# Wider stretches in a channel mix: one row of 512-column stretches over all batches, and a token mix cut 512, 512, 64

## The chip, the cores and the metric

The kernel runs on one core of one Trainium2 chip. The metric is the device time of one execution in microseconds; the median of three runs stands for a kernel. TensorE is called PE below, VectorE DVE, ScalarE ACT, GpSimd POOL, and SyncE, which issues the transfers, SP.

## What is computed

A linear attention whose feature map is a product of two small projections, followed by an MLP mixer (4 batches, 4 heads, 1088 tokens, 32 per head, so 128 channels):

```python
def phi(x):                                   # r = 8, r*r = 64 features
    a = np.einsum('rd,bhsd->bhsr', S1, x)
    b = np.einsum('rd,bhsd->bhsr', S2, x)
    return np.einsum('bhsi,bhsj->bhsij', a, b).reshape(*x.shape[:-1], r * r)
q_p, k_p = phi(q), phi(k)
kv = np.einsum('bhsf,bhsd->bhfd', k_p, v);  z = np.sum(k_p, axis=2)
x = num / den                                 # q_p @ kv over q_p @ z + 1e-6, as (batch, 1088, 128)

h = np.maximum(x.transpose(0, 2, 1) @ w_tok1, 0.0) @ w_tok2    # 1088 -> 256 -> 1088
u = x + h.transpose(0, 2, 1)
h2 = np.maximum(u @ w_ch1, 0.0) @ w_ch2                        # 128 -> 1536 -> 128
return u + h2
```

The weights arrive as 64-bit doubles.

## The kernel before, in words

**Numbers.** The doubles come in as pieces (`pieces[w, i]`, w = 0, 1 for the two token weights, 2, 3 for the two channel weights). `convert` turns a piece into 32-bit words: ACT splits off two parts into scratch tiles `c` and `tail` (512 columns, 4 buffers each), DVE takes three steps (L424, L428, L431), POOL adds (L435 `whole`, L437). `divide_weight` then makes a high half (ACT, L524) and a low half (POOL, L527) in `halves`. Most matmuls work on such halves: three matmuls, high x high, low x high, high x low, in place of one. Batch 0's token mix uses the unsplit words in full precision (L866, L988) and needs no halves.

**Work of one batch.** `keys`: projections of k (L554), products on DVE (L584), sums over tokens (L601). `queries_on_pe` (batch 0) or `queries_by_dma` (the others; projection L747, a way through DRAM, products on POOL L790). `mixing`: attention (L810), division on DVE, the split of x into `xh` (ACT, L834) and `xl` (POOL, L838), the first token weight (L866 or L872), relu, a transpose (L906), and the second token weight by chunks of columns, `CHUNKS`: 384, 384 and 320 (L988 for batch 0, on top of the transposed x of L897; L992 for the others, with the sum `us` made on DVE, L1008, from x transposed through DRAM). `evict` splits the sum u into `uh` (ACT, L963) and `ul` (DVE or POOL, L966).

**Channel mix.** The columns of u are taken in stretches, `SPANS`. Batch 0 has three of its own, the chunks; the other 3264 columns are one row of seven stretches of 384, one of 320 and one of 256, which may cross from one batch into the next. A stretch i has 12 blocks, one for each 128 of the 1536 hidden channels. A block is: `U{i}.f`, three matmuls into a `ps_h` bank (L1042); relu on ACT into `hh` (L1046); the low half `hl` on DVE (L1049); `U{i}.s`, three matmuls that add into a `ps_o` bank (L1055). After the last block DVE adds u (L1074, L1080) and SP stores. `SEGS` says in which order batch 0's blocks of its three stretches follow each other. All `.f` are in one fixed order, and all `.s`. Four `hid` buffers, three `ps_h`, two `ps_o` and four `u` buffers lie between the steps; a stretch is `WIDE` = 384 columns at most.

**Order.** `Plan` is a list scheduler that runs while the kernel is built: each operation has a cost for each engine that can do it, and among those that could start first, the one of highest level is emitted next. The level is the longest chain of costs behind it, plus `BOOST` by batch, plus a hand-set rank in `LEAD`. Where the plan sees PE without work, `fill` puts in 128-wide dummy matmuls on `ident` (L396). Buffers are modelled by `Hold`s. SP issues all transfers in the emitted order, at first in that of `LOADS`.

Of the kernel before, what the change touches and what calls it, by code (L numbers as in the profile page):

```python
# [10 lines left out]
F32R = mybir.dt.float32r  # L11
# [7 lines left out]
P = 128  # L19
# [8 lines left out]
CHUNKS = ((0, 384), (384, 384), (768, 320))  # L28
# [5 lines left out]
LOADS = "k0 q0 00 v0 01 02 03 04 10 11 20 30 q1 12 13 k1 21 31 v1 14 15 22 32".split()  # L34


WIDE = 384


def _spans():  # L40
    spans = [((0, c0, cn),) for c0, cn in CHUNKS]
    at = S
    for n in (384,) * 7 + (320, 256):
        parts = []
        while n:
# [11 lines left out]
SEGS = ((0, 0, 3), (1, 0, 3), (0, 3, 6), (1, 3, 6), (0, 6, 12), (1, 6, 12), (2, 0, 12))  # L57
assert sorted((i, e) for i, a, z in SEGS for e in range(a, z)) == [(i, e) for i in range(len(CHUNKS)) for e in range(NCH)]
# [7 lines left out]
    "A0.d0": -55300.0,  # L66
    "A0.d2": -2900.0,
    "A0.hT": 99500.0,
    "A0.n0": 59800.0,
    "A0.u1": 66400.0,  # L70
    "A0.u2": 63900.0,
    "A0.ul00": 51100.0,
    "A0.w2": 98700.0,
    "A0.x0": 29300.0,
    "A1.t0": -21500.0,
    "A1.t2": 16200.0,
    "A1.w0": -1423700.0,
    "A1.w2": 149000.0,
    "A1.x": 36300.0,
    "A2.n0": 110900.0,  # L80
    "A2.n1": 30300.0,
    "A2.n2": 115300.0,
    "A2.t2": -9900.0,
    "A2.uh05": -52300.0,
    "A2.uh06": -48100.0,
    "A2.w1": -147500.0,
    "A2.w2": -7500.0,
    "A3.hT": 82300.0,
    "A3.n0": 18000.0,
    "A3.t1": 40600.0,  # L90
    "A3.t2": 52300.0,
    "A3.uh09": 12800.0,
    "A3.us1": 38200.0,
    "A3.w0": -35900.0,
    "A3.w1": 2000.0,
    "A3.xb": -47500.0,
    "K0.c0": 184300.0,
    "K0.kvz": -17600.0,
    "K0.s14": 36100.0,
    "K0.s18": 52100.0,  # L100
    "K0.v8": -11500.0,
    "K1.c0": 73400.0,
    "K1.c8": -25000.0,
    "K1.p": 67100.0,
    "K1.s": 38100.0,
    "K1.v4": -86800.0,
    "K1.v8": -128900.0,
    "K2.p": -75625.5,
    "K2.s": 10700.0,
    "K3.p": 82600.0,  # L110
    "Q0.a00": 152400.0,
    "Q0.a01": 23200.0,
    "Q0.a11": -165700.0,
    "Q0.a20": 154800.0,
    "Q0.b01": 29200.0,
    "Q0.b11": -8100.0,
    "Q0.b21": 27500.0,
    "Q0.p0": 54300.0,
    "Q0.p2": 48700.0,
    "Q1.m00": 6600.0,  # L120
    "Q1.m01": -5000.0,
    "Q1.m10": 32900.0,
    "Q1.m11": -14900.0,
    "Q1.p": 2300.0,
    "Q2.p": 10200.0,
    "Q3.p": -69800.0,
    "U0.f": 780300.0,
    "U0.ol": 14800.0,
    "U1.f": 96700.0,
    "U1.oh": 52400.0,  # L130
    "U10.f": 900.0,
    "U11.f": 1400.0,
    "U2.f": -4000.0,
    "U4.f": 1480700.0,
    "U5.f": 163600.0,
    "U6.f": 150900.0,
    "U7.f": 35100.0,
    "w00.hi": -193600.0,
    "w00.lo": -296700.0,
    "w00.low": 6200.0,  # L140
    "w01.hi": -700.0,
    "w01.lo": -62200.0,
    "w02.clamp": 45400.0,
    "w02.lo": -1516300.0,
    "w02.low": 60300.0,
    "w02.shift": -5600.0,
    "w03.abs": -1200.0,
    "w03.add": -25300.0,
    "w03.hi": -52900.0,
    "w03.lo": -45700.0,  # L150
    "w03.merge": -189600.0,
    "w04.abs": 70300.0,
    "w04.clamp": 120900.0,
    "w04.hi": -95600.0,
    "w04.lo": -148800.0,
    "w04.low": 12100.0,
    "w04.merge": -96000.0,
    "w10.abs": 40900.0,
    "w10.hi": 9100.0,
    "w10.low": 19600.0,  # L160
    "w10.merge": 60000.0,
    "w11.abs": 27600.0,
    "w11.clamp": 23000.0,
    "w11.hi": -196900.0,
    "w11.lo": 183000.0,
    "w11.low": -2900.0,
    "w11.shift": -682900.0,
    "w12.abs": 42900.0,
    "w12.hi": -107800.0,
    "w12.lo": -27700.0,  # L170
    "w12.low": 159700.0,
    "w12.merge": 3100.0,
    "w13.abs": 21600.0,
    "w13.add": 1100.0,
    "w13.clamp": -55300.0,
    "w13.hi": 23500.0,
    "w14.clamp": 17900.0,
    "w14.lo": 33800.0,
    "w14.low": -113600.0,
    "w15.abs": -800.0,  # L180
    "w15.clamp": 34000.0,
    "w15.low": -82500.0,
    "w20.abs": 10900.0,
    "w20.add": -18200.0,
    "w20.low": 4400.0,
    "w21.abs": -10800.0,
    "w21.clamp": 74900.0,
    "w21.lo": -14000.0,
    "w22.lo": 4700.0,
    "w22.low": -175100.0,  # L190
    "w30.abs": -6400.0,
    "w30.lo": 12000.0,
    "w30.merge": 75500.0,
    "w30.shift": -68200.0,
    "w31.abs": -10200.0,
    "w31.clamp": 3800.0,
    "w31.hi": 16200.0,
    "w32.abs": -5300.0,
    "w32.add": 3600.0,
    "w32.clamp": 700.0,  # L200
    "w32.low": -289100.0,
# [140 lines left out]
def act_sb(n):  # L342
    return {"act": 100 + 0.834 * n}
# [15 lines left out]
def attn_mixer_kernel(ctx: ExitStack, tc: tile.TileContext, qT, kT, v1, s64, wt1, wt2, wc1, wc2, out):  # L359
# [46 lines left out]

    def convert(name, raw, n, loaded, dst=None, keep=None):
# [7 lines left out]
        def magnitude(_):  # L415
            t["c"] = const.tile([P, n], I32, name="s_c") if keep else new("c", [P, CONV], I32)[:, :n]
            nc.scalar.activation(f32(t["c"]), f32(high), AF.Abs)  # L417

        def rest(_):
            t["tail"] = new("tail", [P, CONV], I32)[:, :n]  # L420
            nc.scalar.activation(t["tail"], low.bitcast(U32), AF.Copy, scale=2.0 ** -29)  # L421
# [28 lines left out]
    for w, (src, sizes) in enumerate((  # L450
        (wt1, [n * DTOK for n in CUTS[0]]), (wt2, [cn for _, cn in CHUNKS for _ in range(2)]), (wc1, [n * P for n in CUTS[2]]), (wc2, [n * P for n in CUTS[3]]),
    )):
        for i, n in enumerate(sizes):
            pieces[w, i] = src[:, sum(sizes[:i]):sum(sizes[:i + 1])]
# [209 lines left out]
    def queries_on_pe(qp_hold):  # L664
# [16 lines left out]
        for g, (c0, cn) in enumerate(CHUNKS):  # L681
# [112 lines left out]
    def mixing(b, kvz_done, qp_done, qp_hold, boost, free):  # L794
# [5 lines left out]
        for g in range(3):  # L800
# [49 lines left out]
            if b:  # L850
                m = plan.add(f"{n}.h{g}", act_sb(384), high, [m], [xs_hold] if g == 0 else (), [x_hold] + ([xs_hold] if g else []), boost, order=split[:1])
                m = plan.add(f"{n}.l{g}", either(384), low, [m], (), [x_hold, xs_hold], boost, port=True)
# [37 lines left out]
        def residual(i, after):  # L890
# [10 lines left out]
            return plan.add(f"{n}.u{i}", {"pe": 3 * 109.0}, emit, [divided[i]], [u_banks[i]], [x_hold], boost, order=after)  # L901
# [75 lines left out]
        for i, (c0, cn) in enumerate(CHUNKS):  # L977
# [3 lines left out]
            def second(_, i=i, c0=c0, cn=cn):  # L981
# [4 lines left out]
                for f in range(2):  # L986
                    if not b:
                        nc.tensor.matmul(u_ps[:, :cn], lhsT=t["hTh"][:, f, :], rhs=f32(whole[1, 2 * i + f])[:, :cn], start=False, stop=(f == 1), skip_group_check=True)  # L988
                        continue
                    for l, r in (("hTh", 0), ("hTh", 1), ("hTl", 0)):  # L990
                        k += 1
                        nc.tensor.matmul(u_ps[:, :cn], lhsT=t[l][:, f, :], rhs=part(1, 2 * i + f, r, 0, cn), start=(k == 1), stop=(k == 6))  # L992
# [3 lines left out]
                [m] + ([] if b else [residuals[i]]) + [(is_split if b else is_whole)[1, 2 * i + f] for f in range(2)],  # L996
# [3 lines left out]
            if b:  # L1000
# [26 lines left out]
    def channel_mix(segs):  # L1027

        o_holds, outs = {}, {}
        for i, e0, e1 in segs:  # L1030
# [3 lines left out]
            for e in range(e0, e1):  # L1034
# [22 lines left out]
                cost = 3 * cn * 0.453  # L1057
# [104 lines left out]
```

## Time and profile before

| | |
|---|---|
| median of 3 runs | 223.22 us (222.94 to 223.72) |
| span of the profiled execution | 220.9 us |
| PE busy, share of the span | 215.2 us, 97% |
| DVE, ACT, POOL busy | 138.2, 118.8, 79.7 us |
| data moved | 28.42 MB, mean 129 GB/s |

The span goes from the first instruction to the last; the run's time has a little more around it. PE busy counts each matmul from its start to its modelled end, and matmuls overlap, so that the mean of one is longer than the interval between two. The chain that ended last is followed back from the last instruction, at each step to what released it; its pieces give start, duration, engine, tile, line and, after an x, the number of instructions. In the tables of groups, `out<-in`, shapes and count are followed by busy us, the mean ns of one, and the engine's idle time before them with what ended it.

### The profile page before, as it was taken

To read this page: it belongs to the slowest core of one execution; us is meant where nothing else is said; L and a number is where in the kernel's file an instruction comes from. 1 tells how busy PE (TensorE), PEld (TensorE's weight loads), DVE (VectorE), ACT (ScalarE), POOL (GpSimd) and SP (SyncE) were. 2 spreads that over 40 slices of the span, in tenths; PEclk is the share of its full clock that TensorE was granted. 3 is DMA by queue.
4 is the path that set the end of the run, shared out by engine and by line. 5 is a ranking of instruction groups with operands and counts; after the bars stand their busy time and mean duration, and the time that the engine had idled before them with its cause. 6 is when DMAs were issued, how large, how long until landed. Compare 5 with 4: busy or idle time off the path is not lost.

```text
span 220.9 us, 4955 instructions
## 1 busy us (share of the span) xinstructions
PE 215.2 (97%) x1906; PEld 203.5 (92%) x1906; DVE 138.2 (63%) x273; ACT 118.8 (54%) x284; POOL 79.7 (36%) x85
## 2 busy tenths in 40 slices
PE   7999989999999999999999999999999999999994
PEld 7878768889998999999999999999999999999993
DVE  1689899888578466554934454658256556556562
ACT  4586799996554344542632554455234543545451
POOL 2074588989999101920500220464002200100000
PEclk9999999999999999999999999999999999999999
DMA  5999995984005997400170267500610100000000
GB/s 202 386 410 409 407 401 183 203 184 152 1 3 194 254 233 157 156 3 0 39 214 0 65 141 173 150 1 4 213 36 0 40 0 4 32 3 36 0 33 24
DMA packets 11351, 28.42 MB, mean 129 GB/s; under 512 B 1472, under 2 KB 5568, under 8 KB 11328
## 3 DMA queue, kind: packets, MB, share of 16 engines
q1 hardware_dynamic: 11328, 28.11, 41.1%
q8 instruction: 15, 0.25, 0.5%
q14 instruction: 8, 0.07, 0.1%
HBM read 23.27 MB, written 4.83 MB: 127 GB/s over the span
## 4 chain that ended last, share of the span: by engine, by line
PE 82%; ACT 7%; DMA 5%; SPq 2%; issue 2%; DVE 0%; ACTq 0%
PE ps_o L1055 31%; PE ps_h L1042 31%; DMA doubles<-wt 5%; PE ps_a L872 4%; PE ps_a L810 4%; PE ps_a L992 4%; PE ps_a L601 2%; SPq L400 2%; ACT halves L524 2%; PE ps_a L554 2%; ACT hh L1046 1%; ACT c L417 1%; PE ps_a L866 1%; ACT tail L421 1%; PE ps_a L988 1%
## 5 line engine op out<-in xcount | busy, mean ns | idle before, releaser
L1049 DVE SCALAR_TENSOR_TENSOR hl<-ps_h,hh 128x384 fp32r<-128x384 f32 (+2 forms) x144 | 75.4, 534 | 52.2 <-ACT hh L1046 46.5
L1046 ACT ACTIVATE hh<-ps_h 128x384 fp32r<-128x384 f32 (+2 forms) x144 | 68.0, 477 | 58.5 <-PE ps_h L1042 33.2
L1042 PE MATMUL ps_h<-uh,halves 128*128 128x384 f32 (+2 forms) x288 | 89.0, 334 | 0.2
L1055 PE MATMUL ps_o<-hh,halves 128*128 128x384 f32 (+2 forms) x288 | 71.3, 330 | 0.0
L1042 PEld LDWEIGHTS ps_h<-uh,halves 128*128 128x128 f32 x288 | 53.3, 188 | 2.6 <-DVE hl L1049 1.0
L1055 PEld LDWEIGHTS ps_o<-hh,halves 128*128 128x128 f32 x288 | 50.5, 188 | 0.2
L1055 PE MATMUL ps_o<-hl,halves 128*128 128x384 f32 (+2 forms) x144 | 47.4, 329 | 0.0
L1042 PE MATMUL ps_h<-ul,halves 128*128 128x384 f32 (+2 forms) x144 | 47.4, 329 | 0.0
L966 POOL TENSOR_TENSOR ul<-us,uh 128x64 fp32r<-128x64 f32 (+4 forms) x15 | 9.7, 655 | 64.7 <-ACT uh L963 64.6
L1055 PEld LDWEIGHTS ps_o<-hl,halves 128*128 128x128 f32 x144 | 27.1, 188 | 0.3 <-DVE hl L1049 0.3
L1042 PEld LDWEIGHTS ps_h<-ul,halves 128*128 128x128 f32 x144 | 27.1, 188 | 0.2
L790 POOL TENSOR_TENSOR qp<-qp,br 128x544 f32<-128x544 f32 x12 | 16.2, 1369 | 11.5 <-PE ps_o L1055 8.2
L584 DVE TENSOR_TENSOR k_p<-ps_a,a_sb 128x1024 f32<-128x1024 f32 (+1 forms) x12 | 11.1, 952 | 7.6 <-ACT a_sb L564 7.6
L838 POOL TENSOR_TENSOR xl<-x,xh 128x384 fp32r<-128x384 f32 x9 | 9.0, 1012 | 14.1 <-ACT xh L834 11.3
L435 POOL TENSOR_TENSOR whole<-c,tail 128x512 int32<-128x512 int32 (+3 forms) x11 | 11.6, 1058 | 4.3 <-DVE c L431 2.8
L396 PEld LDWEIGHTS ps_o<-ident 128*128 128x128 f32 x68 | 10.0, 224 | 3.3 <-issue 1.5
L396 PE MATMUL ps_o<-ident 128*128 128x128 f32 x68 | 11.2, 319 | 1.4 <-POOL ident masks.py:199 1.4
L421 ACT ACTIVATE tail<-doubles 128x512 int32<-128x512 uint32 (+3 forms) x17 | 10.6, 630 | 3.2 <-DMA doubles<-wt 1.7
L527 POOL TENSOR_TENSOR halves<-whole,halves 128x384 fp32r<-128x384 f32 (+3 forms) x11 | 11.4, 1058 | 0.0
L417 ACT ACTIVATE c<-doubles 128x512 f32<-128x512 f32 (+3 forms) x17 | 10.1, 616 | 1.3 <-POOL whole L435 1.0
L431 DVE SCALAR_TENSOR_TENSOR c<-doubles,ps_h 128x512 int32<-128x512 int32 (+3 forms) x17 | 10.2, 611 | 0.1
L428 DVE TENSOR_SCALAR ps_h<-c 128x512 int32<-128x512 int32 (+3 forms) x17 | 10.1, 617 | 0.2
(76 smaller groups left out, 231.4 us busy)
## 6 DMA issues: line engine op xcount, KB each, us to landing
qp<-rows SPq DMA_DIRECT2D x6, 544.0 KB, 8.8
br<-rows SPq DMA_DIRECT2D x12, 272.0 KB
doubles<-wc SPq DMA_DIRECT2D x6, 512.0 KB
v_sb<-v SPq DMA_DIRECT2D x4, 594.0 KB
q_sb<-qT SPq DMA_DIRECT2D x4, 544.0 KB, 12.7
doubles<-wt SPq DMA_DIRECT2D x4, 512.0 KB, 7.8
k_sb<-kT SPq DMA_DIRECT2D x3, 576.0 KB, 5.9
xm<-xb SPq DMA_DIRECT2D x3, 576.0 KB, 2.8
```

Source lines behind the costliest of these rows:

```text
L396: nc.tensor.matmul(spare_ps[:, :P], lhsT=ident, rhs=ident, start=True, stop=True)
L417: nc.scalar.activation(f32(t["c"]), f32(high), AF.Abs)
L421: nc.scalar.activation(t["tail"], low.bitcast(U32), AF.Copy, scale=2.0 ** -29)
L431: nc.vector.scalar_tensor_tensor(t["c"], high, -(1 << 30), t["ps"], op0=ALU.bitwise_and, op1=ALU.bitwise_or)
L435: engines[e].tensor_tensor(dst(), t["c"], t["tail"], op=ALU.add)
L527: engines[e].tensor_tensor(halves[w, i][:, 1], f32(whole[w, i] if w < 2 else t["c"]), f32(halves[w, i][:, 0]), op=ALU.subtract)
L584: engines["pool" if on_pool else "dve"].tensor_tensor(t["k_p"][:pn, t0 * H:t1 * H], a.unsqueeze(3).broadcast_to([pn, n, R, R]), t["sb", t0 ...
L790: engines[e].tensor_tensor(qp[:, p, cs], qp[:, p, cs], t["br"][:, p, cs], op=ALU.mult)
L1042: nc.tensor.matmul(h_ps[:, :cn], lhsT=part(2, at[2][e][0], l, at[2][e][1] * P, P), rhs=r[:, :cn], start=(m == 0), stop=(m == 2))
L1046: nc.scalar.activation(t["hh"][:, :cn], t["h"][:, :cn], AF.Relu)
L1049: nc.vector.scalar_tensor_tensor(t["hl"][:, :cn], t["h"][:, :cn], 0.0, f32(t["hh"][:, :cn]), op0=ALU.max, op1=ALU.subtract)
L1055: nc.tensor.matmul(outs[i][:, :cn], lhsT=part(3, at[3][e][0], l, at[3][e][1] * P, P), rhs=r[:, :cn], start=(e == 0 and m == 0), stop=(e == ...
```

## The change

- `CHUNKS` becomes 512, 512, 64 (token mix), while batch 0's queries keep their old cut as `QUERIES`. The second token weight comes in four pieces of 512 columns and one of 128 that holds both halves of the last chunk (`at1`), instead of four of 384 and two of 320; the load `15` goes.
- `SPANS` is one row over the columns of all batches: eight stretches of 512, then 256. The third (columns 1024 to 1535) holds 64 columns of batch 0 and 448 of batch 1. `SEGS` orders the blocks of the first two. `WIDE` is 512.
- For batches 1 to 3 `evict` makes one piece for each stretch and batch, after all the sums (`us`) it covers, instead of one for each chunk, stretch and batch.
- The scratch `c` and `tail` has no buffers of its own any more: slots of the tiles `us`, `xh` and `xl` are lent to it. Batch 1's first `xh` and first `us` are ordered after all conversions (`finished`).
- Batch 0's transposed x of chunk 0 follows the second division instead of the first (4, 4 and 1 transposes instead of 3 each).
- The plan's cost of a half block is 3 (cn / 2.4 + 14) instead of 3 x 0.453 cn, and `LEAD` is a new table: 62 entries in place of 136.

```diff
-CHUNKS = ((0, 384), (384, 384), (768, 320))
+CHUNKS = ((0, 512), (512, 512), (1024, 64))
+QUERIES = ((0, 384), (384, 384), (768, 320))
...
-WIDE = 384
+WIDE = 512
...
-    spans = [((0, c0, cn),) for c0, cn in CHUNKS]
-    at = S
-    for n in (384,) * 7 + (320, 256):
+    spans, at = [], 0
+    for n in (512,) * 8 + (256,):
...
-SEGS = ((0, 0, 3), (1, 0, 3), (0, 3, 6), (1, 3, 6), (0, 6, 12), (1, 6, 12), (2, 0, 12))
+SEGS = ((0, 0, 3), (1, 0, 3), (0, 3, 6), (1, 3, 6), (0, 6, 12), (1, 6, 12))
...
+    used = {"c": 0, "tail": 0}
+    lent = {}
+
+    def slot_of(kind, n):
+        i = used[kind] % 4
+        used[kind] += 1
+        if (kind, i // 2) not in lent:
+            if kind == "c":
+                lent[kind, i // 2] = new("us", [P, S]).bitcast(I32)
+            else:
+                lent[kind, i // 2] = new("xh" if i < 2 else "xl", [P, NT, P], F32R).rearrange("p t c -> p (t c)").bitcast(I32)
+        return lent[kind, i // 2][:, i % 2 * CONV:i % 2 * CONV + n]
...
-        (wt1, ...), (wt2, [cn for _, cn in CHUNKS for _ in range(2)]), ...
+        (wt1, ...), (wt2, [512] * 4 + [128]), ...
...
+    def at1(i, f):
+        return (4, f * 64) if i == 2 else (2 * i + f, 0)
...
+    finished = list(is_split.values()) + list(is_whole.values())
...
-                ... order=split[:1])
+                ... order=split[:1] or (finished if b == 1 else []))
...
-            return plan.add(f"{n}.u{i}", {"pe": 3 * 109.0}, emit, [divided[i]], ...)
+            return plan.add(f"{n}.u{i}", {"pe": (4, 4, 1)[i] * 109.0}, emit, [divided[(1, 2, 2)[i]]], ...)
...
-            for k, parts in enumerate(SPANS):
-                d0 = 0
-                for pb, p0, pn in parts:
-                    lo, n_ = max(c0, p0), min(c0 + cn, p0 + pn) - max(c0, p0)
-                    if pb == b and n_ > 0:
-                        evict(k, i, s, lo - c0, d0 + lo - p0, n_)
-                    d0 += pn
+            if not b:
+                evict(i, i, [s], 0, 0, cn)
+        for k, parts in enumerate(SPANS if b else ()):
+            d0 = 0
+            for pb, p0, pn in parts:
+                if pb == b:
+                    evict(k, None, [puts[i] for i, (c0, cn) in enumerate(CHUNKS) if c0 < p0 + pn and p0 < c0 + cn], p0, d0, pn)
+                d0 += pn
...
-                cost = 3 * cn * 0.453
+                cost = 3 * (cn / 2.4 + 14.0)
```

More of the change, by code (lines that the diff above doesn't have):

```diff
@@ L33 @@
 CUTS = {0: (2, 2, 2, 2, 1), 2: (4, 4, 4), 3: (4, 4, 4)}
-LOADS = "k0 q0 00 v0 01 02 03 04 10 11 20 30 q1 12 13 k1 21 31 v1 14 15 22 32".split()
-WIDE = 384
+LOADS = "k0 q0 00 v0 01 02 03 04 10 11 20 30 q1 12 13 k1 21 31 v1 14 22 32".split()
+WIDE = 512
 def _spans():
-    spans = [((0, c0, cn),) for c0, cn in CHUNKS]
-    at = S
-    for n in (384,) * 7 + (320, 256):
+    spans, at = [], 0
+    for n in (512,) * 8 + (256,):
         parts = []
@@ L55 @@
 SPANS = _spans()
-SEGS = ((0, 0, 3), (1, 0, 3), (0, 3, 6), (1, 3, 6), (0, 6, 12), (1, 6, 12), (2, 0, 12))
-assert sorted((i, e) for i, a, z in SEGS for e in range(a, z)) == [(i, e) for i in range(len(CHUNKS)) for e in range(NCH)]
+SEGS = ((0, 0, 3), (1, 0, 3), (0, 3, 6), (1, 3, 6), (0, 6, 12), (1, 6, 12))
+assert sorted((i, e) for i, a, z in SEGS for e in range(a, z)) == [(i, e) for i in range(2) for e in range(NCH)]
 HID = 4
@@ L65 @@
 LEAD = {
[L66 to L201, printed above, removed]
+    "A0.d2": -106500.0,
+    "A0.u0": -892000.0,
+    "A0.uh2": 603600.0,
+    "A0.ul2": 16800.0,
+    "A1.d2": 103200.0,
+    "A1.hT": -683700.0,
+    "A1.x": 88900.0,
+    "K1.s": -130900.0,
+    "K2.c0": -96100.0,
+    "K2.p": 22100.0,
+    "K2.s": -1744800.0,
@@ new lines @@
+    "Q0.a01": 114300.0,
+    "Q0.a10": 138700.0,
+    "Q0.a11": 1111800.0,
+    "Q0.a20": 182200.0,
+    "Q0.b11": 59200.0,
+    "Q0.m11": -23800.0,
+    "Q0.p0": 318100.0,
+    "Q0.p1": 233900.0,
+    "Q1.p": 123800.0,
+    "Q3.p": -274800.0,
+    "U0.h": 443800.0,
+    "U0.l": -264800.0,
+    "U0.s": -46700.0,
+    "U1.s": -1079000.0,
+    "U4.s": 355100.0,
+    "U6.s": -53300.0,
+    "U8.f": 163400.0,
+    "w00.hi": -183800.0,
+    "w01.lo": -253800.0,
+    "w02.abs": -44500.0,
+    "w02.lo": -282600.0,
@@ new lines @@
+    "w03.abs": 823000.0,
+    "w03.low": -54400.0,
+    "w03.shift": -975800.0,
+    "w04.hi": 382200.0,
+    "w10.clamp": 2800.0,
+    "w10.hi": 423600.0,
+    "w10.low": -84800.0,
+    "w11.shift": -221100.0,
+    "w12.abs": 248700.0,
+    "w12.clamp": 6400.0,
+    "w13.add": -225300.0,
+    "w13.lo": -1255900.0,
+    "w13.low": -209500.0,
+    "w14.add": -311900.0,
+    "w20.clamp": 576900.0,
+    "w20.hi": -45900.0,
+    "w21.abs": -61700.0,
+    "w21.lo": 49200.0,
+    "w21.low": 24000.0,
@@ L202 @@
+    "w22.clamp": -120700.0,
+    "w22.lo": -355900.0,
+    "w22.low": -217900.0,
+    "w30.abs": 188100.0,
+    "w30.clamp": 99400.0,
+    "w31.abs": -83500.0,
+    "w31.low": -130800.0,
+    "w31.shift": -7800.0,
+    "w32.abs": -4974600.0,
+    "w32.clamp": -56900.0,
+    "w32.low": -672300.0,
 }
@@ L415, in magnitude @@
         def magnitude(_):
-            t["c"] = const.tile([P, n], I32, name="s_c") if keep else new("c", [P, CONV], I32)[:, :n]
+            t["c"] = const.tile([P, n], I32, name="s_c") if keep else slot_of("c", n)
             nc.scalar.activation(f32(t["c"]), f32(high), AF.Abs)
         def rest(_):
-            t["tail"] = new("tail", [P, CONV], I32)[:, :n]
+            t["tail"] = slot_of("tail", n)
             nc.scalar.activation(t["tail"], low.bitcast(U32), AF.Copy, scale=2.0 ** -29)
@@ L450, in attn_mixer_kernel @@
     for w, (src, sizes) in enumerate((
-        (wt1, [n * DTOK for n in CUTS[0]]), (wt2, [cn for _, cn in CHUNKS for _ in range(2)]), (wc1, [n * P for n in CUTS[2]]), (wc2, [n * P for n in CUTS[3]]),
+        (wt1, [n * DTOK for n in CUTS[0]]), (wt2, [512] * 4 + [128]), (wc1, [n * P for n in CUTS[2]]), (wc2, [n * P for n in CUTS[3]]),
     )):
@@ L680, in queries_on_pe @@
         done = {}
-        for g, (c0, cn) in enumerate(CHUNKS):
+        for g, (c0, cn) in enumerate(QUERIES):
             a_holds, b_holds = [Hold("ps_a") for _ in range(2)], [Hold("ps_h") for _ in range(2)]
@@ L850, in mixing @@
             if b:
-                m = plan.add(f"{n}.h{g}", act_sb(384), high, [m], [xs_hold] if g == 0 else (), [x_hold] + ([xs_hold] if g else []), boost, order=split[:1])
+                m = plan.add(f"{n}.h{g}", act_sb(384), high, [m], [xs_hold] if g == 0 else (), [x_hold] + ([xs_hold] if g else []), boost, order=split[:1] or (finished if b == 1 else []))
                 m = plan.add(f"{n}.l{g}", either(384), low, [m], (), [x_hold, xs_hold], boost, port=True)
@@ L900, in emit @@
                     )
-            return plan.add(f"{n}.u{i}", {"pe": 3 * 109.0}, emit, [divided[i]], [u_banks[i]], [x_hold], boost, order=after)
+            return plan.add(f"{n}.u{i}", {"pe": (4, 4, 1)[i] * 109.0}, emit, [divided[(1, 2, 2)[i]]], [u_banks[i]], [x_hold], boost, order=after)
         def transpose(_):
@@ L951, in mixing, with evict @@
         second_done, puts = [], []
-        def evict(k, i, s, src, dst, cn):
-            c0 = CHUNKS[i][0]
+        def evict(k, i, after, src, dst, cn):
             def columns():
-                return box["us", b][:, c0 + src:c0 + src + cn] if b else t["u", i][:, src:src + cn]
+                return box["us", b][:, src:src + cn] if b else t["u", i][:, src:src + cn]
             def high(_):
@@ L970, in evict @@
             of = us_hold if b else u_banks[i]
-            hi = plan.add(f"{n}.uh{i}{k}", act_sb(cn) if b else act(cn), high, [s], [u_hold] if first else (), [of] + ([] if first else [u_hold]), boost, order=u_first.get(k, ()))
+            hi = plan.add(f"{n}.uh{k}", act_sb(cn) if b else act(cn), high, after, [u_hold] if first else (), [of] + ([] if first else [u_hold]), boost, order=u_first.get(k, ()))
             u_first.setdefault(k, [hi])
-            u_done.setdefault(k, []).append(plan.add(f"{n}.ul{i}{k}", either(cn) if b else dve(cn), low, [hi], (), [of, u_hold], boost, port=b > 0))
+            u_done.setdefault(k, []).append(plan.add(f"{n}.ul{k}", either(cn) if b else dve(cn), low, [hi], (), [of, u_hold], boost, port=b > 0))
             if b:
@@ L987, in second @@
                     if not b:
-                        nc.tensor.matmul(u_ps[:, :cn], lhsT=t["hTh"][:, f, :], rhs=f32(whole[1, 2 * i + f])[:, :cn], start=False, stop=(f == 1), skip_group_check=True)
+                        nc.tensor.matmul(u_ps[:, :cn], lhsT=t["hTh"][:, f, :], rhs=f32(whole[1, at1(i, f)[0]])[:, at1(i, f)[1]:at1(i, f)[1] + cn], start=False, stop=(f == 1), skip_group_check=True)
                         continue
@@ L991, in second @@
                         k += 1
-                        nc.tensor.matmul(u_ps[:, :cn], lhsT=t[l][:, f, :], rhs=part(1, 2 * i + f, r, 0, cn), start=(k == 1), stop=(k == 6))
+                        nc.tensor.matmul(u_ps[:, :cn], lhsT=t[l][:, f, :], rhs=part(1, at1(i, f)[0], r, at1(i, f)[1], cn), start=(k == 1), stop=(k == 6))
             s = plan.add(
                 f"{n}.w{i}", {"pe": 6 * (cn / 2.4 + 14) if b else 4 * (cn / 1.2 + 3)}, second,
-                [m] + ([] if b else [residuals[i]]) + [(is_split if b else is_whole)[1, 2 * i + f] for f in range(2)],
+                [m] + ([] if b else [residuals[i]]) + [(is_split if b else is_whole)[1, j] for j in sorted({at1(i, f)[0] for f in range(2)})],
                 [u_banks[i]] if b else (), [hTs_hold] + ([] if b else [u_banks[i]]), boost, order=second_done[-1:] if b else (),
@@ L1011, in put @@
                             )
-                s = plan.add(f"{n}.us{i}", dve(cn), put, [s] + moved, [] if i else [us_hold], [u_banks[i], xT_hold] + ([us_hold] if i else []), boost, order=puts[-1:])
+                s = plan.add(f"{n}.us{i}", dve(cn), put, [s] + moved, [] if i else [us_hold], [u_banks[i], xT_hold] + ([us_hold] if i else []), boost, order=puts[-1:] or (finished if b == 1 else []))
                 puts.append(s)
-            for k, parts in enumerate(SPANS):
-                d0 = 0
-                for pb, p0, pn in parts:
-                    lo, n_ = max(c0, p0), min(c0 + cn, p0 + pn) - max(c0, p0)
-                    if pb == b and n_ > 0:
-                        evict(k, i, s, lo - c0, d0 + lo - p0, n_)
-                    d0 += pn
+            if not b:
[6 more added lines that the diff above has]
+                d0 += pn
         return second_done, residuals[2:] if not b else second_done[2:]
```

## The prediction

> **What bounds the kernel now.** I read the page first: engine shares, the clock row, the shares of the chain that ended last.
>
> ```profile
> span 220.9 us, 4955 instructions
> PE 215.2 (97%) x1906; PEld 203.5 (92%) x1906; DVE 138.2 (63%) x273; ACT 118.8 (54%) x284; POOL 79.7 (36%) x85
> ...
> PEclk9999999999999999999999999999999999999999
> ...
> PE 82%; ACT 7%; DMA 5%; SPq 2%; issue 2%; DVE 0%; ACTq 0%
> ```
>
> PE is the bound and its granted clock never falls, so the price of the change is the sum of what PE's instructions take from start to start, plus the times at which PE has nothing to do. The groups' mean durations don't give that price, because matmuls overlap. The chain in order of time does: in its unbroken stretches, first and last piece and the number of matmuls between them give the interval of each width. L1042 and L1055 are the two halves of the channel mix, L992 the token mix of batches 1 to 3, L988 that of batch 0.
>
> ```profile
> 171.01 0.53 PE ps_o L1055 x3
> ...
> 184.79 0.53 PE ps_o L1055 x3
> ...
> 186.37 0.88 PE ps_a L992 x6
> ...
> 187.25 0.52 PE ps_h L1042 x3
> ...
> 197.13 0.52 PE ps_o L1055 x3
> ...
> 199.57 0.88 PE ps_h L1042 x6
> ...
> 207.49 0.44 PE ps_o L1055 x3
> ...
> 210.69 0.35 PE ps_h L1042 x3
> ...
> 215.97 1.77 PE ps_o L1055 x15
> ...
> 217.76 0.42 DVE o_sb L1080
> ```
>
> From 171.01 to 184.79 lie 78 matmuls of 384 columns, 176.7 ns each; from 187.25 to 197.13 lie 57, 173.3 ns each. So the same shape has two paces. From 199.57 to 207.49: 54 of 320 columns, 146.7 ns. From 210.69 to 215.97: 45 of 256 columns, 117.3 ns. The step from 320 to 384 columns in neighbouring stretches is 26.6 ns for 64 columns, 0.416 ns a column, which leaves 13.5 ns fixed per matmul at 320 and, at 384, 13.6 or 17.0 ns.
>
> Where the saturated part begins (first line, from PE's timeline), and what PE does in it beside the channel mix (from the chain):
>
> ```profile
> 33.42 0.63 PE L1042 MATMUL ps_h<-uh,halves 128*128 128x384 f32 x1
> ...
> 30.20 1.31 PE ps_a L988 x4
> ...
> 59.38 1.08 PE ps_a L988 x4
> ...
> 62.03 2.26 PE ps_a L810 x72
> 66.57 0.63 PE ps_a L747 x16
> ...
> 72.75 3.23 PE ps_a L872 x27
> 75.98 2.25 PE ps_a L601 x72
> 78.23 1.05 PE ps_a L554 x36
> ...
> 82.28 1.06 PE ps_a L992 x6
> ...
> 86.00 1.93 PE ps_a L992 x12
> ```
>
> The channel mix is 12 blocks of 6 matmuls, 72, per stretch: nine stretches of 384, two of 320, one of 256. With 175 ns as the mean of the two paces that is 648 x 0.175 + 144 x 0.1467 + 72 x 0.1173 = 113.4 + 21.1 + 8.4 = 142.9 us. The other PE work after 33.42 is, for three batches each, 2.26 + 2.25 + 3.23 + 2.99 (L992: 1.06 + 1.93), plus two each of 0.63 and 1.05, plus 1.08 and about 1 of transposes: 37.6. Together 180.5 us, against 217.74 - 33.42 = 184.3 that passed. So PE loses only about 4 us after its first channel-mix matmul, and the end is that start, plus the work, plus 4, plus a tail of one 0.42 us addition and a store, which both kernels share (the last stretch is 256 wide in both). The execution profiled spans 220.9; the median run is 223.22, so I carry 2.3 us outside the span over unchanged.
>
> **The change, part by part.**
>
> *Wider stretches.* Twelve stretches become eight of 512 and one of 256: 648 channel-mix matmuls instead of 864, over the same columns. No row shows a 512-column matmul of this kind. Upper end: the steepest step between rows, 117.3 to 146.7 for 64 columns, is 0.46 ns a column and carried from 320 gives 235 ns. Then 576 x 0.235 + 8.4 = 143.8, a loss of 0.9. Middle: 0.416 ns a column from the two paces of 384 gives 226.6 and 230.0. Lower end: the full-precision matmuls of batch 0 reload 128 columns of weights each time too, and seem to pay no fixed part:
>
> ```profile
> L866 PE MATMUL ps_a<-whole,x 128*128 128x256 f32 x18 | 4.6, 395 | 0.0
> ...
> 23.43 1.03 PE L866 MATMUL ps_a<-whole,x 128*128 128x256 f32 x4
> ```
>
> Four in 1.03 us, the last one 0.395 long: (1.03 - 0.395) / 3 = 212 ns from start to start, which is 256 columns at twice 0.416. If the fixed part is hidden as soon as the array streams for 213 ns, 512 columns take 213 ns. I take the middle, 228.3, because it is what the same instruction shows at the nearest width: 576 x 0.2283 + 8.4 = 139.9, **-3.0 us**.
>
> The Trainium skill, TensorE: Matmul & The Clock Gate, section Wait — 56ns, not 53.3ns?, puts the gap of warm back-to-back matmuls at N / 2.4 + about 2.5 ns, 215.7 measured at N = 512. At 384 it would be 162.5, where the rows have 173.3 and 176.7, so the trace does not agree with it at that width; the estimate for the channel mix by it would be 576 x 0.2157 + 8.4 = 132.7, -10.2 us instead of -3.0.
>
> *Token mix in 512, 512, 64.* For batches 1 to 3 L992 has 18 matmuls as before. The 64-wide ones are the doubtful price: each still loads 128 weight columns. The nearest row is 256 wide at 117.3, with the same load, and no row is narrower; by 0.416 a column plus 13.5 it would be 40. I take 117, the row: per batch 12 x 0.2283 + 6 x 0.117 = 3.44 against 2.99, **+1.35 us** for three batches (-0.05 with 40 ns). Batch 0: two chunks of 4 matmuls at 1.31 x 512/384 = 1.74 and one of 4 short ones, about 0.54 by the row below, 4.0 against 1.31 + 1.31 + 1.08 = 3.7: **+0.3**.
>
> ```profile
> 20.33 1.09 PE ps_o L396 x8
> ```
>
> (128-wide full-precision matmuls with a load each, 136 ns.)
>
> *The start.* U0's first matmul at 33.42 follows this chain: POOL's rebuilding of the first two pieces of the second token weight, four matmuls, an ACT copy, a DVE subtraction.
>
> ```profile
> 27.84 1.98 POOL L435 TENSOR_TENSOR whole<-c,tail 128x384 int32<-128x384 int32 x2 [1.33 <-ACT tail L421]
> ...
> 31.54 0.48 ACT L963 CAST uh<-ps_a 128x384 fp32r<-128x384 f32 x1 [0.39 <-PE ps_a L988]
> ...
> 32.49 0.55 DVE L966 TENSOR_TENSOR ul<-ps_a,uh 128x384 fp32r<-128x384 f32 x1
> ...
> L435 POOL TENSOR_TENSOR whole<-c,tail 128x512 int32<-128x512 int32 x4 | 5.1, 1283 | 1.2 <-DVE c L431 1.1
> ...
> L431 DVE SCALAR_TENSOR_TENSOR c<-doubles,ps_h 128x512 int32<-128x512 int32 x10 | 6.8, 682 | 0.1
> ```
>
> Each piece becomes 512 wide: POOL 2 x 1.283 - 1.98 = +0.6, PE +0.43, ACT about +0.12, DVE +0.13 (0.682 at 512 against 0.55): 1.3 us later, of which 0.43 is in the sum already: **+0.8**. If the new ranks put this chain ahead of other conversions it is 0, and the loads of those two pieces bring at most 0.26 MB more ahead of it. The new ranks are otherwise costed at nothing: what covers them is that PE has channel-mix blocks to fall back on; if that cover ends it is the starvation rival below. One load less on SP's queue and the lent buffers (conversion scratch in the later `us`, `xh`, `xl`) are also costed at nothing: their new order makes batch 1's first `xh` follow all conversions, and L872, which needs that `xh`, waits anyway for weights that POOL finishes last (row under the first rival).
>
> *Fewer hand-offs.* 144 blocks become 108, each with one ACT relu and one DVE subtraction.
>
> ```profile
> L1049 DVE SCALAR_TENSOR_TENSOR hl<-ps_h,hh 128x384 fp32r<-128x384 f32 x108 | 59.0, 555 | 42.7 <-ACT hh L1046 37.1 <-PE ps_o L1055 4.9
> L1046 ACT ACTIVATE hh<-ps_h 128x384 fp32r<-128x384 f32 x108 | 52.8, 495 | 45.8 <-PE ps_h L1042 24.5 <-PE ps_o L1055 20.8
> ```
>
> Both ride beside PE (0.555 and 0.495 in a block of 1.05) and stay so (some 0.68 and 0.61 in 1.37). Of the 4 us lost I let the share of the blocks shrink: **-0.7**, bounded by 0 and by a quarter of 4, 1.0. Longer blocks also give the weight conversions, on which the first blocks wait, more time.
>
> Sum: -3.0 + 1.35 + 0.3 + 0.8 - 0.7 = -1.25; 223.2 - 1.25 = **222.0 us**.
>
> **The rivals.**
>
> *PE starves at the third stretch (slower).* Before, a 320-wide stretch of batch 0 alone fills PE while batch 1 is prepared; now the third stretch needs batch 1.
>
> ```profile
> 67.13 0.41 PE L1042 MATMUL ps_h<-uh,halves 128*128 128x320 f32 x1
> ...
> 88.22 0.34 PE L1042 MATMUL ps_h<-uh,halves 128*128 128x384 f32 x1
> ...
> 68.71 3.23 POOL L527 TENSOR_TENSOR halves<-whole,halves 128x256 fp32r<-128x256 f32 x3
> ```
>
> That filler is 72 x 0.1467 = 10.6 us between 67.13 and 88. Now PE has 24 blocks of 1.37 = 32.9 us and about 17.5 us of other work (rows of the third fence: 2.26, 2.25 twice, 3.23, 0.63, 1.05 twice, the 3.44 and 0.54 above, some 0.7 of transposes) from some 34.6, enough until about 85. Batch 1's chain could be done at 81.4: POOL's weights end at 71.94, L872 ends at 75.98, then relu, transpose, split, six matmuls, `us`, `uh`, `ul`, some 5.4 us. It decides from 85 on; as late as before, with the first matmul at 88.22, it would cost about 3 us: 225.0. For it: L992's first six only start at 82.28 now; against it: nothing pressed them to.
>
> *Width is paid by the column.* At 235 ns the sum is -1.25 + (576 + 36) x 0.0067 = +2.9: 226.1. For it: 256 to 320 rises by 0.46. Against: 320 to 384 by 0.416 in the neighbouring stretch.
>
> *The fixed part is hidden at 512.* At 213 ns: 222.0 - 612 x 0.015 = 212.8. For it the full-precision row; against it that the fixed part of this kind does not shrink from 256 to 384. The Trainium skill's gap (TensorE: Matmul & The Clock Gate, the section named above) would end near the same, 2.5 ns later per matmul, an estimate of 214.
>
> *Cheap short matmuls and the better pace.* 40 ns for the 64-wide ones (-1.4) and 226.6 for 512 (612 x 0.0017 = -1.0): 219.6.
>
> **How the numbers follow.** Forecast 0.52, its own range 220.5 to 223.2; starvation 0.13; by the column 0.13; hidden 0.09; cheap 0.13. Faster by over 0.3% (about what a measurement here can tell from no change) means under 222.55: 0.8 of the forecast (0.42) and the two fast cases (0.22) make 0.64, of which I move 0.06 up for the unseen order of the new ranks: 0.58. Same 0.17: the forecast's upper end with the 0.06. Slower 0.25: the two slow cases. The range 218.0 to 225.8 takes in the cheap case and starvation and leaves out the hidden case and the far part of by-the-column.
>
> **What would show it.** After: groups of three 512-wide matmuls 0.68 to 0.69 us apart in the chain (0.64 for hidden, 0.705 for by the column); six 64-wide L992 in 0.70 (0.24 if cheap); the first L1042 near 34.6; no gap of PE before the third stretch, between 80 and 90; L1049 and L1046 near 0.68 and 0.61. Wrong if PE's chain breaks at a batch border, or if the width has another price than 228.

## The result and the profile after

The change made the kernel slower: 225.5 us (median of 6 runs, 224.68 to 226.49) against 223.48 (6 runs beside it), ratio 1.0105, 95% interval 1.0082 to 1.0129. The prediction had 222.0.

The page of the kernel after:

```profile
span 222.9 us, 4355 instructions
PE 217.0 (97%) x1696; PEld 177.7 (80%) x1696; DVE 134.1 (60%) x228; ACT 112.1 (50%) x239; POOL 79.5 (36%) x77
...
PEclk9999999999999999999999999999999999999999
...
PE 84%; DMA 11%; DVE 2%; SPq 1%; issue 1%
```

PE issues 210 matmuls fewer and is busy no less (217.0 us against 215.2); its granted clock is the same. The chain in order of time (L984 and L997 are the halves of the channel mix, L933 the token mix of batches 1 to 3):

```profile
37.50 1.59 PE ps_h L984 x6
...
85.31 3.39 PE ps_a L933 x18
...
139.57 0.59 PE ps_a L933 x6
...
160.84 1.39 PE ps_a L933 x6
...
163.64 0.70 PE ps_o L997 x3
...
177.00 0.69 PE ps_h L984 x3
...
219.85 0.42 DVE o_sb L1022
```

From 163.64 to 177.00 lie 57 matmuls of 512 columns, 234.4 ns each: twice the 117.3 of 256 columns, to within 0.2 ns. The six 64-wide ones take 0.59, 98 ns each. The other engines' steps came as forecast, 689 and 600 ns:

```profile
L991 DVE SCALAR_TENSOR_TENSOR hl<-ps_h,hh 128x512 fp32r<-128x512 f32 x96 | 65.6, 689 | 59.1 <-ACT hh L988 56.7 <-PE ps_o L997 1.7
L988 ACT ACTIVATE hh<-ps_h 128x512 fp32r<-128x512 f32 x96 | 57.6, 600 | 65.3 <-PE ps_h L984 45.8 <-PE ps_o L997 12.8 <-DVE us L949 3.7
```

The account in the prediction's manner. Channel mix: 576 x 0.2344 + 8.4 = 143.4 us, +0.5. Token mix of batches 1 to 3: 3 x 3.39 against 3 x 2.99, +1.2. Batch 0's: 1.72 twice and 0.39, +0.1. So PE has 1.8 us more to do, and the end lies 219.85 - 217.76 = 2.1 later: all but 0.3 is work.

### The profile page after: what moved, and what is told of

Same layout as the page of the kernel before. It is cut to its first block, busy times and chain, and to the rows that moved or that the text cites. A ratio compares the mean times of both kernels' runs of the same rounds, so it can differ in the third digit from the quotient of the medians.

```text
span 222.9 us, 4355 instructions
## 1 busy us (share of the span) xinstructions
PE 217.0 (97%) x1696; PEld 177.7 (80%) x1696; DVE 134.1 (60%) x228; ACT 112.1 (50%) x239; POOL 79.5 (36%) x77
## 4 chain that ended last, share of the span: by engine, by line
PE 84%; DMA 11%; DVE 2%; SPq 1%; issue 1%
PE ps_h L984 33%; PE ps_o L997 32%; PE ps_a L933 5%; DMA doubles<-wc 5%; PE ps_a L815 4%; DMA doubles<-wt 4%; DMA v_sb<-v 3%; PE ps_a L753 3%; PE ps_a L544 3%; PE ps_a L497 1%; PE ps_a L929 1%; PE ps_o L322 1%; SPq L326 1%; PE ps_a L690 1%; DVE k_p L527 1%
## 5 line engine op out<-in xcount | busy, mean ns | idle before, releaser
L991 DVE SCALAR_TENSOR_TENSOR hl<-ps_h,hh 128x512 fp32r<-128x512 f32 (+1 forms) x108 | 70.5, 660 | 61.6 <-ACT hh L988 59.2
L988 ACT ACTIVATE hh<-ps_h 128x512 fp32r<-128x512 f32 (+1 forms) x108 | 62.0, 576 | 69.7 <-PE ps_h L984 47.4
L984 PE MATMUL ps_h<-uh,halves 128*128 128x512 f32 (+1 forms) x216 | 78.6, 388 | 0.0
L997 PE MATMUL ps_o<-hh,halves 128*128 128x512 f32 (+1 forms) x216 | 65.6, 386 | 0.0
L984 PEld LDWEIGHTS ps_h<-uh,halves 128*128 128x128 f32 x216 | 40.4, 188 | 8.9 <-DVE hl L991 0.2
L997 PEld LDWEIGHTS ps_o<-hh,halves 128*128 128x128 f32 x216 | 39.0, 188 | 8.4 <-issue 0.4
L997 PE MATMUL ps_o<-hl,halves 128*128 128x512 f32 (+1 forms) x108 | 41.4, 383 | 0.0
L984 PE MATMUL ps_h<-ul,halves 128*128 128x512 f32 (+1 forms) x108 | 41.4, 383 | 0.0
L997 PEld LDWEIGHTS ps_o<-hl,halves 128*128 128x128 f32 x108 | 20.3, 188 | 4.3
L984 PEld LDWEIGHTS ps_h<-ul,halves 128*128 128x128 f32 x108 | 20.4, 188 | 4.2 <-issue 0.2
L356 ACT ACTIVATE us<-doubles 128x512 f32<-128x512 f32 (+2 forms) x16 | 10.4, 655 | 4.4 <-DMA doubles<-wt 1.6
L466 POOL TENSOR_TENSOR halves<-whole,halves 128x512 fp32r<-128x512 f32 (+2 forms) x10 | 11.5, 1168 | 1.6 <-ACT halves L463 1.6
(79 smaller groups left out, 237.3 us busy)
```

The costliest lines, as they stand in the source:

```text
L466: engines[e].tensor_tensor(halves[w, i][:, 1], f32(whole[w, i] if w < 2 else t["c"]), f32(halves[w, i][:, 0]), op=ALU.subtract)
L984: nc.tensor.matmul(h_ps[:, :cn], lhsT=part(2, at[2][e][0], l, at[2][e][1] * P, P), rhs=r[:, :cn], start=(m == 0), stop=(m == 2))
L988: nc.scalar.activation(t["hh"][:, :cn], t["h"][:, :cn], AF.Relu)
L991: nc.vector.scalar_tensor_tensor(t["hl"][:, :cn], t["h"][:, :cn], 0.0, f32(t["hh"][:, :cn]), op0=ALU.max, op1=ALU.subtract)
L997: nc.tensor.matmul(outs[i][:, :cn], lhsT=part(3, at[3][e][0], l, at[3][e][1] * P, P), rhs=r[:, :cn], start=(e == 0 and m == 0), stop=(e == ...
```

## The experiments

**What does a column cost?** Theory, made after the result: time goes by the column, 0.458 ns in this kind of matmul (234.4 / 512), and the number of matmuls is free down to a floor set by the weight load. Rival: 13.5 ns for each matmul, as predicted. The first two kernels cut the matmuls; since the parts of a bank are started separately, parts of the sums are lost, and only the time is read.

```diff
-  nc.tensor.matmul(h_ps[:, :cn], lhsT=..., rhs=r[:, :cn], ...)
+  c = 0
+  for w in CUT.get(i, (cn,)):
+      nc.tensor.matmul(h_ps[:, c:c + w], lhsT=..., rhs=r[:, c:c + w], ...)
+      c += w
```

> The kernel after, every 512-wide matmul of the channel mix cut into two of 256, 576 more matmuls and weight loads, everything else the same. By the column: 2 x 117.3 = 234.6 ns against 234.4, so 225.5 us within 0.5. With 13.5 ns for each matmul: 576 x 0.0135 = 7.8 us more, 233.

Measured: 227.31 us, ratio to before 1.0179 (1.0127 to 1.0231). Its chain:

```profile
105.21 0.71 PE ps_h L987 x6
...
113.04 0.71 PE ps_o L1003 x6
```

Eleven half blocks in 7.83 us, 0.712 each: 2 x 118.6 = 237.3 ns where one matmul took 234.4. So 576 more matmuls and weight loads cost some 1.7 us, not 7.8: 2.9 ns each. The rival falls; between 256 and 512 columns the theory is right but for those 3 ns. They are a mean. Later in the same kernel the pace is another:

```profile
187.13 2.16 PE ps_h L987 x18
...
210.89 1.44 PE ps_h L987 x12
```

Here lie 198 matmuls of 256 columns, 120.0 ns each, and the last stretch, whose matmuls are not cut, takes 0.36 a half block too, where the kernel after has 0.35. So one width has several paces, as 384 had in the kernel before, and no run here shows what sets them.

> The kernel after, with each matmul of the channel mix cut into narrower ones inside the same stretch, each with its own weight load: stretch 2 as 2 x 256, stretch 3 as 4 x 128, stretch 4 as 8 x 64, stretch 5 as 320 + 192, stretch 6 as 384 + 128; the others stay 512. Read from the chain: the time of one half block (uncut: 0.70 us). Theory (time goes by the column, 0.458 ns, with a floor of some 98 ns set by the weight load, from the 64-wide token mix matmuls at 0.59 / 6): 0.70, 1.18, 2.36, 0.73, 0.82 us. Rival of the prediction (0.416 ns a column and 13.5 ns for each matmul, no floor): 0.72, 0.80, 0.96, 0.72, 0.72 us.

Measured in one execution: 345.58 us, of which only the chain is of use.

```profile
127.35 1.34 PE ps_h L987 x12
...
151.58 2.60 PE ps_h L987 x24
...
195.97 15.36 PE ps_h L987 x72
...
281.90 0.77 PE ps_h L987 x6
...
310.18 0.86 PE ps_h L987 x6
```

The pieces are 4 x 128 (111.7 ns a matmul), 8 x 64 (at first 24 in 2.60, 108.3, later 72 in 15.36, 213.3), 320 + 192 (0.77) and 384 + 128 (0.86). The theory had 1.18, 2.36, 0.73 and 0.82 for a half block, the rival 0.80, 0.96 and 0.72 twice; the theory is nearer in each, and too low. With 146.7 at 320 and 175 at 384 the narrow partners are left 110 and 112. So in a stream below about 240 columns (110 / 0.458) a matmul takes 108 to 112 ns whatever its width, and the weight load that each of them has is the likely bound. The floor of 98 was too low; that six short ones between wide ones get part of a load hidden would fit, and is not shown. The 213.3 is twice 106.7, and the windows of that kernel say why:

```profile
124.67:146.11 21.44, 21.44 (x195) 21.44 (x193) 5.53 (x9) 4.78 (x8) 0.78 (x1) 1.00 0.00 1
195.97:211.32 15.35, 15.35 (x74) 15.29 (x76) 1.38 (x2) 1.19 (x2) 0.00 (x0) 0.50 0.00 0
```

(The columns are the window, its length, PE, PEld, DVE, ACT and POOL busy, the granted clock, DMA.) In the later stream of 64-wide matmuls the clock was granted at 0.50, though PE counts as busy throughout.

**What is the tenth above 0.416 ns?** Two kernels: one with 16-bit operands in the channel mix, one without the DVE step beside it.

```diff
-  t["hh"], t["hl"] = new("hh", [P, WIDE], F32R), new("hl", [P, WIDE], F32R)
+  t["hh"], t["hl"] = new("hh", [P, WIDE], BF16), new("hl", [P, WIDE], BF16)
...   (uh, ul and the halves of the two channel weights in the same way)
```

> The kernel after with the operands of the channel mix (uh, ul, hh, hl and the halves of its weights) kept in 16-bit floats instead of the rounded 32-bit ones; it keeps fewer bits of each product. If the tenth above 0.416 ns a column belongs to the 32-bit operands, a 512-wide matmul takes some 213 to 216 ns and the time falls by 576 x 0.0185 = 10.7 us, to about 214.8 (the Trainium skill, TensorE: Matmul & The Clock Gate, gives 215.7 ns for 512 columns). If it belongs to the array, to PSUM or to what the other engines do beside it, the interval stays 234 and the time stays within 1 us of 225.5.

Measured: 213.67 us, ratio 0.9571 (0.9541 to 0.9600).

```profile
157.57 0.65 PE ps_h L985 x3
...
169.23 0.65 PE ps_h L985 x3
```

Eighteen half blocks in 11.66 us: 215.9 ns for 512 columns. The Trainium skill, TensorE: Matmul & The Clock Gate, section Wait — 56ns, not 53.3ns?, has N / 2.4 + about 2.5 ns, 215.7 at N = 512. The trace agrees for 16-bit operands and does not for rounded 32-bit ones, where it has 234.4.

> The kernel after without the DVE step of the channel mix (the low half hl is left out; the third matmul of the second half block reads hh instead), 108 DVE instructions of 128x512 and 70 us of DVE work less. If the tenth above 0.416 ns a column comes from other engines reading and writing the same memories beside PE, the half block of 512 falls below 0.70 us, to as little as 0.65 (the 16-bit run's pace). If it belongs to the 32-bit operands, it stays 0.70, and only hand-offs get shorter, 225 within 1.

Measured in one execution: 225.23 us, with 222.88 for the kernel before.

```profile
104.53 0.70 PE ps_h L984 x3
...
111.56 0.71 PE ps_h L984 x3
```

Ten half blocks in 7.03 us: 234.3 ns, with half of DVE's work gone (66.6 us busy in place of 134.1). So DVE's step isn't the cause. The 16-bit kernel also halves what ACT and DVE write beside PE; against that as the cause stands the end of the kernel after, where ACT has nothing left to do and DVE pauses from 219.17 to its last addition at 219.85:

```profile
218.75 0.42 DVE L991 SCALAR_TENSOR_TENSOR hl<-ps_h,hh 128x256 fp32r<-128x256 f32 x1 [0.28 <-ACT hh L988]
...
219.19 0.28 PE L997 MATMUL ps_o<-hl,halves 128*128 128x256 f32 x1
...
219.54 0.28 PE L997 MATMUL ps_o<-hl,halves 128*128 128x256 f32 x1
```

The three intervals of 256 columns in this pause still take 117 ns each. What is left is the operands' kind. How the array or its reads come to a tenth more with these operands no run here shows.

**Is it PE's work that sets the time?**

```diff
                         k += 1
+                        if i == 2 and k > 1:
+                            continue
```

> The kernel after, leaving out five of the six 64-wide token mix matmuls of batches 1 to 3 (so the last 64 tokens of these batches get only one of six products); the order of all else is the same. Theory (PE's work sets the time, and a 64-wide matmul costs the 98 ns of its weight load): 15 x 0.098 = 1.5 us less, 224.0. Rival (they fill time in which PE would wait anyway): 225.5 within 0.4.

Measured: 223.47 us (12 runs), ratio to before 1.0036 (1.0014 to 1.0059), where the kernel after stood at 1.0105.

```profile
85.34 2.83 PE ps_a L935 x13
```

Against 3.39 with all 18: 0.56 less per batch, 1.7 for three, and the ratio falls by 0.007, 1.5 us. What is taken off PE's chain comes off the time.

> The kernel before with the channel mix's operands in 16-bit floats, fewer bits of each product kept, as in the run of the kernel after that took 213.67. With 0.416 ns a column and 2.5 ns for each matmul (215.8 ns at 512 there) the channel mix takes 130.6 + 864 x 0.0025 = 132.7 us instead of 142.9: 223 - 10.2 = 212.8, so the change is 0.9 slower in this form too, since 216 matmuls less save only 0.5 there. If narrow matmuls keep a fixed 13 ns with 16-bit operands, 222.

Measured: 213.26 us, ratio 0.9552 (0.9509 to 0.9596), not told apart from the kernel after in the same form (0.9571). Forecast was 212.8.

```profile
164.91 0.49 PE ps_h L1043 x3
...
175.15 0.49 PE ps_o L1056 x3
```

These are 63 matmuls of 384 columns, 162.5 ns each, where the 32-bit ones had two paces, 173.3 and 176.7. Against 215.9 at 512 that is 0.417 ns a column and some 2.4 fixed, so with 16-bit operands a split into a rate and a fixed part holds. Where a matmul is its columns plus 2.5 ns, 216 matmuls fewer are worth 0.5 us, which the 1.2 us more of the token mix would take back; the runs can't resolve that.

> The kernel before with 16-bit operands in the channel mix and in the token mix of batches 1 to 3 as well (fewer bits of each product kept). At 0.416 ns a column and 2.5 ns a matmul the token mix saves 81 x 0.010 + 36 x 0.0125 + 18 x 0.011 = 1.5 us against the run with the channel mix alone (213.26): 211.8. If weight loads of 16-bit operands bind at 256 columns, no gain.

Measured: 211.33 us, ratio 0.9479 (0.9466 to 0.9493), the fastest of all, with fewer bits of each product kept: 1.9 below the run before, 1.6 by the two ratios, forecast 1.5.

**Lent scratch, ranks, start.**

```diff
-            t["c"] = ... new("c", [P, CONV], I32)[:, :n]
+            t["c"] = ... slot_of("c", n)
...   (tail likewise; batch 1's first xh and us ordered after the conversions)
```

> The kernel before with one part of the change alone: the conversion scratch lent from us, xh and xl, and batch 1's first xh and us ordered after all conversions; widths, ranks and plan costs of before. If lending is free, 223 within 0.7. If the shared tiles tie conversions together or push the order about, some of the 4 us by which the channel mix of the kernel after starts later shows here: the first L1042-like matmul after 35 us instead of 33.4, and 225 or more. The run with stretches of 512 had this part too (230.05): what this run takes above 223 is not owed to the width there.

Measured: 222.54 us, ratio 0.9966 (0.9944 to 0.9988), first channel-mix matmul at 33.76. Lending is free.

> The kernel before with stretches of 512 (five, then 448 and 256) instead of 384 for the columns after batch 0, and with the lent scratch of the kernel after to make room; token mix, batch 0's stretches, ranks and plan costs stay those of before. By the column the channel mix costs the same as before, so the time is 223.5 within 1 (fewer hand-offs may give 0.5, ranks no longer fitted may take 1). If wider stretches as such made the kernel after slower, 225 or more. If they saved a fixed part, 221.

Measured: 230.05 us, ratio 1.0309 (1.0238 to 1.0379). The number falls under "225 or more", but the reason named there, wider stretches as such, is not what the trace shows. A half block of 512 takes 0.70, as elsewhere, and the end (the last addition on DVE) comes at 224.49, 6.7 later than before. Most of that is lost early, in batch 0's stretches, which are still 384 wide:

```profile
54.50 0.63 PE L1056 MATMUL ps_h<-uh,halves 128*128 128x384 f32 x2 [0.95 <-POOL halves L540]
...
56.11 0.69 PE L1056 MATMUL ps_h<-uh,halves 128*128 128x384 f32 x1 [0.64 <-DVE us L444]
...
50.00:62.00 12.00, 10.20 (x45) 8.73 (x44) 6.55 (x13) 5.70 (x12) 11.69 (x11) 0.86 0.22 73
...
56.20:59.40 3.20, 3.20 (x10) 3.02 (x11) 2.68 (x6) 1.45 (x3) 3.01 (x3) 0.50 0.00 0
...
180.72:188.65 7.93, 7.75 (x37) 6.11 (x37) 5.12 (x9) 4.01 (x8) 3.01 (x4) 1.00 0.09 34
```

The kernel before, in the first of these windows:

```profile
50.00:62.00 12.00, 12.00 (x69) 11.43 (x67) 7.87 (x17) 7.44 (x17) 11.80 (x12) 1.00 0.21 68
```

From 50 to 62 us PE has 45 matmuls, where the kernel before has 69: 24 fewer, at 175 ns an estimate of 4.2 us. PE waits there for POOL and DVE, which are still converting weights, and after that its granted clock is 0.50 for some 3 us. Why the conversions come later in this order no run here shows; the lent scratch alone does not do it (the run above). At the borders between stretches the chain leaves PE too:

```profile
180.72 1.07 PE ps_a L1006 x6
181.81 0.57 DVE us L1022
...
184.06 0.75 PE ps_h L1056 x2
...
186.27 2.38 PE ps_h L1056 x9
```

Of the 4.5 us from 181.8 to 186.3 only 0.75 are PE's in the chain. But PE is busy for 7.75 of the 7.93 us around it (the row from 180.72), so this border costs tenths of a microsecond. PE does starve in this run, but mostly for weights, and not at a batch border as my rival had it.

The same run has a width that no other has, the stretch of 448 columns:

```profile
203.74 0.60 PE ps_h L1056 x3
...
204.97 0.36 PE L1056 MATMUL ps_h<-ul,halves 128*128 128x448 f32 x1
...
213.34 0.60 PE ps_h L1056 x3
```

From 203.74 to 213.34 lie 48 matmuls, 200.0 ns each: 0.446 a column, not 0.458. So the theory by the column is not exact either; 0.416 a column and the 13.5 ns of the prediction give 199.9 here. At this pace all columns of the channel mix would take some 140 us in place of 142.9, an estimate (4352 x 72 x 0.446 ns), which no run tried.

> The kernel after with an empty rank table. It and its twin (the kernel before with an empty table) tell the structure from the ranks. Theory (the structure brings 1.7 us more PE work, the ranks of both kernels only remove waits): both get slower, this one by 5 to 15 us, 230 to 240. Rival (the new ranks are a poor fit and made the kernel after slow): 225.5 or less.

> The kernel before with an empty rank table: 228 to 238 by the theory that its ranks are worth as much as those of the kernel after. If it stays near 223, the old ranks were worth nothing and the structure alone made the difference.

Measured: 231.02 (ratio 1.0362, 1.0342 to 1.0383) and 230.4 (1.0333, 1.0314 to 1.0352). Each table of ranks is worth 5.5 to 7.4 us to its own kernel; without them the new structure stands 0.6 us above the old, and the intervals overlap. By these two runs alone the new ranks could still be the poorer fit, by up to the 1.9 us between 5.5 and 7.4; against it speaks that with them PE loses 1.4 us after its start, and 3.8 in the kernel before (worked out below).

> The kernel after with the order at its start changed: POOL rebuilds and splits the first piece of the first channel weight before that of the second, and the sums of batch 1's keys wait on PE until the first channel-mix block is issued. Theory (the start is late by order, not by width): the first channel-mix matmul moves from 37.5 to about 35, PE's dummy matmuls and idle time before it shrink by up to 2 us, the time falls by 1 to 2, to 224. Rival (the start does not matter because PE has other work meanwhile, or the rest of the order suffers): 225.5 within 0.7.

Measured: 234.61 us, ratio 1.0497 (1.0458 to 1.0537). The edit didn't do what it was for: the first channel-mix matmul came at 37.59, and later PE waited for a channel weight that POOL now split late.

```profile
PE ps_h L987 <- POOL halves L469: 3.7, 1, 3.7
...
74.60:81.20 6.60, 4.17 (x14) 3.74 (x15) 1.38 (x2) 1.19 (x2) 6.60 (x7) 0.50 0.61 193
```

(The second row is a window that begins in that wait; the clock in it is granted at 0.50.) It says how much one shift of order can cost, and nothing on the start, which was not tried in another way.

## Why the prediction was wrong

**The step that failed** is the price of a 512-wide matmul, "I take the middle, 228.3": it measured 234.4. The term for the channel mix was -3.0 and came out +0.5: 3.5 us off, where the whole sum was 3.3 off (-1.25 against +2.0). The other terms nearly cancel. From the rows I had split the interval into 0.416 ns a column and a fixed part, by one step of 64 columns between two stretches, one of which had two paces. All three widths of the rows in one line bear another reading: 117.3, 146.7 and 175 (the mean of the two paces) are 0.456 to 0.458 ns for each of 256, 320 and 384 columns, with nothing fixed, and 234.4 at 512 lies on it. Neither reading is a law: the split I took is right at 448, where the line is 5 ns too high, and short at 512. What 512 columns have that 448 have not, no run here shows; so the step that failed is the price carried to a width that no row had, and the cause of that price stays open. The upper end that I wrote down, 235, had the price, and "width is paid by the column" was the right rival, at 226.1 and a chance of 0.13. What spoke for it, that the fixed part did not shrink but grew with the width, I read as a reason against another rival only. The lower end, 213, was misread: the program has nine full-precision matmuls at L866 and the row has x18, so each leaves two records, and 212 ns is the interval of half a matmul; no price of one 512-wide matmul follows from it. That 225.5 lies inside the stated range, just below its upper end of 225.8, is luck: the range took in a starvation at 225.0, which did not come, and stopped short of the 226.1 of the right rival, and the direction was wrong.

**Token mix**: +1.35 forecast, +1.2 measured, but by two errors: the 64-wide matmuls took 98 ns for 117, the 512-wide ones 234 for 228.

**The start**: forecast 34.6, measured 37.43.

```profile
32.41 1.28 POOL L466 TENSOR_TENSOR halves<-us,halves 128x512 fp32r<-128x512 f32 x1
...
35.93 1.28 POOL L466 TENSOR_TENSOR halves<-us,halves 128x512 fp32r<-128x512 f32 x1 [1.00 <-POOL us L376]
...
35.18 2.32 PE L544 MATMUL ps_a<-v_sb,k_p 128*64 128x66 f32 x72
37.43 0.50 PE L984 MATMUL ps_h<-uh,halves 128*128 128x512 f32 x1
```

POOL split the piece of the second channel weight (32.41) before that of the first (35.93, done at 37.21), which the first block needs. But PE did batch 1's key sums (L544, 2.32) meanwhile, which the kernel before does after its start. After the start it lost only 219.83 - 37.43 - 181.0 = 1.4 us, where the kernel before lost 3.8. (The 181.0 is the work after the start: 180.5 as in the prediction, 0.5 and 1.2 more by the account above, 1.0 more for batch 0's token mix, of which two chunks follow the start here, and 2.25 less for those key sums.) My terms for start and hand-offs, +0.8 and -0.7, were of the wrong size one by one; that their sum, +0.1, stands against +0.3 is luck too.

**Hidden work**: right. In the kernel after nothing came to wait at a batch border, the third stretch started in time, lending cost nothing.

## What to carry to other kernels

Fit the interval of a matmul over all widths that the trace has before splitting it into a fixed part and a rate; if a line through zero fits as well, wider tiles may buy nothing on PE. Then run the one width that you are going to, for the price may not lie on either line: here 448 columns took 0.446 ns each and 512 took 0.458. A narrow remainder, cut to make the rest wide, has a price of its own, 98 ns for 64 columns here. Where PE is the bound, look at what a column costs by the kind of operand before regrouping columns: here 16-bit operands were worth 10 us, with fewer bits of each product kept, and the regrouping minus 2. And when an order is tuned, measure a change of structure in both orders, with and without the ranks, since either table was worth several times the change.

## What the runs showed of the hardware

- Rounded 32-bit operands at a granted clock of 1.00: 117.3 to 120.0 ns at 256 columns, 146.7 at 320, 173.3 or 176.7 at 384, 200.0 at 448, 234.4 at 512, that is 0.446 to 0.469 a column, and 0.458 at 512. 16-bit operands: 162.5 at 384 and 215.9 at 512, and weight loads of 98 ns in place of 188:

```profile
L998 PEld LDWEIGHTS <-halves 128*128 128x128 bf16 x324 | 31.0, 98 | 32.6 <-issue 0.7
```

- A stream of narrow matmuls, each with its own load of 128 rounded 32-bit columns, took 108 to 112 ns a matmul. The Trainium skill, TensorE: Matmul & The Clock Gate, section LDWEIGHTS (loading the stationary operand), gives columns / 1.2 for a load, for 128 columns an estimate of 106.7 ns, which the trace nearly agrees with.
- A long stream of 64-wide matmuls, each with its own load, ran at a granted clock of 0.50, though PE showed no idle time. In two other runs the clock stood at 0.50 for some 3 and 7 us, from the end or the middle of waits of PE for weight conversions on (56.2 to 59.4 with wide stretches in the kernel before, 74.6 to 81.2 with the order at the start changed).
